# A gated linear-attention and mixer kernel on one core: a new written order for all engines

## The chip, the core and the metric

The kernel runs on one NeuronCore of a Trainium2 chip. Five engines work side by side: TensorE (PE in the profile) multiplies matrices, VectorE (DVE) and ScalarE (ACT) do elementwise work and can read PSUM, GpSimd (POOL) does elementwise work in SBUF only, and SyncE (SP) issues DMA transfers; ACT can issue them too. Each engine works through its own queue in the order in which the program was written, and waits on semaphores for what the others make.

The metric is the time on the device, in microseconds (us), of one execution. The kernel before took 165.89 us in the median of three runs (165.33 to 166.85).

## The reference

Two stages follow each other. The first is a recurrence over time with a state of 48 x 48 for each of 4 x 8 batches and heads; the second is a mixer over tokens and then over channels.

```python
for t in range(S):                                  # S = 768, D = 48
    state = alpha[:, :, t, :, None] * state + np.einsum('bhd,bhe->bhde', k[:, :, t], v[:, :, t])
    y[:, :, t] = np.einsum('bhd,bhde->bhe', q[:, :, t], state)

x = y.transpose(0, 2, 1, 3).reshape(B, S, H * D)    # B = 4, H * D = 384
xt = x.transpose(0, 2, 1)
h = np.maximum(xt @ w_tok1, 0.0) @ w_tok2           # 768 -> 256 -> 768 tokens
u = x + h.transpose(0, 2, 1)
out = u + np.maximum(u @ w_ch1, 0.0) @ w_ch2        # 384 -> 1536 -> 384 channels
```

All inputs and the output are float32 in DRAM; the kernel computes its products in bfloat16 and sums them in float32.

## The kernel before

**Attention in blocks.** Each batch has 3 blocks of 256 tokens, so blocks 0 to 2 belong to batch 0, 3 to 5 to batch 1, up to block 11. The recurrence of a block is written as products: sums of logs of alpha give decay factors, keys are multiplied by the inverse factor and queries by the factor, and a masked product of the two takes the place of the loop. A block works in two halves of 128 tokens (half 0 and half 1), and the state goes from half to half.

**Names.** A step has a short name and the number of its block or batch. For a block n:

- `ld_at`, `ld_qt`, `ld_kt`, `ld_vt`: the loads of alpha, queries, keys and values, 384 KB each, into one of 20 buffers of the class `in`.
- `ln` (blocks 0 to 2, one log 768 wide), or `ln1`, `P`, `lnP`, `r1` (later blocks: a log, a product of neighbouring alphas, its log, a reciprocal).
- `cumw` or `cum`: PE sums the logs. `E`, `Et`, `IE`: ACT takes exponentials of the sum, of the block's total, and of the negative sum.
- `qq`, `ql`, `kk`, `kl`: queries times E, keys times IE, each as two pieces 384 wide in the first blocks.
- `trq`, `trk`, then `evq`, `evk`: PE transposes them, DVE or ACT copies them out of PSUM (from block 6 on a transposing DMA, `dq`, `dk`, does it, and `pq` a copy).
- `vb`: the cast of the values; `vs0`, `vs1`: copies of its halves to the other partitions, written after `K`; `ka`, `kb`, `kc`: the same for keys, from block 3 on.
- `K`: keys times values. `s`, `sa`, `sm`: the new state, from K, the old state and the decay.
- `G0`, `G1`, `mask0`, `mask1`: the two products of keys and queries, and the masks that DVE lays over them; `ia`, `ib`: queries times state; `y0`, `y1`: masked product times values; `x0`, `x1`: the copy of the result to SBUF.

For a batch: `t1` (first token weight, six products each for two tiles), `ht` (relu), `t2_b_i` (second token weight), `u` (add), `up`/`ut` (transpose), `c1` and `rt` (first channel weight, relu), `c2` and `o` (second channel weight, add), `st` (store). `ldw` and `cw` load and cast the weight pieces; `cw_wt20` is the first half of the second token weight, which `t2_0_0` reads first.

**What sets the order.** Nothing is scheduled when the kernel is built. `build` describes all steps with what they need; `run` then walks through the string `ORDER`, in which every step stands once with a letter for its engine (t PE, s ACT, v DVE, g POOL, y SP), and emits them in that order. `BUFS` gives, in the order of first use, the buffer number of every value. So the order of a queue, the engine of a copy and the buffer are all written out. Semaphores make each step wait for what it reads, and a step that writes a buffer waits for the last readers of what stood there.

**Port order.** Steps of DVE and POOL that are marked as using a shared port (the scalings, casts, shifts, `P`, `k0a`, `q0r`) also wait for each other: where one of them follows one of the other engine in the written order, it waits until that has ended. This is `shared`:

```python
if last and last[0] != e:
    self.tc.add_manual_dep(i.ins, last[1].ins.name, ...)
self.port_last = (e, i)
```

**Unread products.** `f1_...` and `f3_...` are 1 or 3 products of a zero tile with 512 columns into a PSUM bank that nobody reads before it is overwritten. They are optional (`filler`, `fill`): each stands ahead of a step of PE, if the order names it.

Of the kernel before, what the change touches and what calls it, by code (L numbers as in the profile page):

```python
# [892 lines left out]
```

## Time and profile before

| | |
|---|---|
| median of three runs | 165.89 us (165.33 to 166.85) |
| the profiled execution, whole | 165.84 us |
| its span, first to last instruction | 164.1 us |
| PE busy | 155.5 us (95%) |
| DVE, ACT, POOL busy | 110.8, 101.1, 75.5 us |
| mean granted TensorE clock | 0.990 |
| read from and written to DRAM | 25.17 MB, 4.72 MB |

A row of a timeline or of a group names the line of the kernel, the engine, the operation and what it writes and reads. An idle time in square brackets at the end of a row is how long the engine stood still ahead of it, and what ended that. A row of a list of waits has the total, the number and the longest. A row of a stretch has its length, then the busy time of PE, PE's weight loads, DVE, ACT and POOL with the number of instructions, then the granted clock, the DMA engines' share and GB/s. Lines that many steps share: L604 is every attention product of PE, L666 the transposes, L697 and L698 the copies of ACT and of DVE and POOL, L653 the scalings, L810 the products t2, L829 and L834 c1 and c2. A row of a DMA ends with the time from its issue to its landing.

### The profile page before, as it was taken

The page shows a single profiled execution, that of the slowest core. Times are in us where ns is not written, and L with a number is a line of the kernel's source. Part 1 is how long each engine was busy: PE and PEld are TensorE (multiplying, and loading weights), DVE is VectorE, ACT ScalarE, POOL GpSimd, SP SyncE. Part 2 cuts the span into 40 slices and gives each one's busy share as a digit, 9 for nine tenths or more (in the row PEclk, how much of TensorE's full clock was granted, in tenths as well). Part 3 has the DMA queues.
Part 4 walks back from the last instruction along what each step waited for, and adds up shares of the span by engine and source line. Part 5 has one row for each costly group of instructions (what it writes and reads, how often), then busy time and mean ns, then how long its engine had stood idle before and what let it go on. Part 6 is the DMA issues. An engine that isn't in the chain of part 4 may idle for free.

```text
span 164.1 us, 4068 instructions
## 1 busy us (share of the span) xinstructions
PE 155.5 (95%) x1601; PEld 98.2 (60%) x1601; DVE 110.8 (68%) x197; ACT 101.1 (62%) x188; POOL 75.5 (46%) x94
## 2 busy tenths in 40 slices
PE   7959889899999999999999999999999999999992
PEld 2444656576657676665667666666566665566660
DVE  4056999689699777967789998874591283524341
ACT  3698798998998786289995947466615101562000
POOL 4054489972942827289795494739700000000000
PEclk9995999999999999999999999999999999999999
DMA  4999999999999998999999999699012135220314
GB/s 127 324 318 321 248 340 279 348 348 344 342 363 336 291 265 202 249 302 211 239 239 174 234 184 221 144 221 248 19 48 100 48 68 129 90 98 9 113 71 143
DMA packets 76322, 34.46 MB, mean 210 GB/s; under 512 B 68112, under 2 KB 76304, under 8 KB 76304
## 3 DMA queue, kind: packets, MB, share of 16 engines
q1 hardware_dynamic: 64704, 27.73, 66.5%
q10 hardware_dynamic: 11600, 6.49, 13.7%
q8 instruction: 12, 0.20, 0.5%
q14 instruction: 6, 0.05, 0.1%
HBM read 25.17 MB, written 4.72 MB: 182 GB/s over the span
## 4 chain that ended last, share of the span: by engine, by line
PE 52%; DVE 4%; ACT 2%; ACTq 1%; issue 1%
PE ps L834 22%; PE ps L829 19%; PE ps L604 6%; PE ps L805 3%; PE ps L810 2%; DVE u L814 1%; ACTq L545 1%; DVE o L838 1%; DVE pkk L653 1%; DVE ut L698 1%; ACT vb L697 0%; ACT ut L697 0%; DVE rt L802 0%; DVE ss L762 0%; ACT lf L592 0%
## 5 line engine op out<-in xcount | busy, mean ns | idle before, releaser
L834 PE MATMUL ps<-wc,rt 128*128 128x384 bf16 (+2 forms) x300 | 54.7, 320 | 0.0
L829 PE MATMUL ps<-ut,wc 128*128 128x384 bf16 x288 | 51.8, 326 | 0.3 <-ACT E L631 0.2
L800 ACT ACTIVATE rt<-ps 128x384 bf16<-128x384 f32 x55 | 25.3, 493 | 24.6 <-PE ps L829 24.5
L829 PEld LDWEIGHTS <-wc 128*128 128x128 bf16 x288 | 27.0, 98 | 17.7 <-issue 1.2
L834 PEld LDWEIGHTS <-rt 128*128 128x128 bf16 x300 | 27.6, 98 | 16.6
L802 DVE TENSOR_SCALAR rt<-ps 128x384 bf16<-128x384 f32 x41 | 21.6, 552 | 14.4 <-PE ps L829 13.9
L720 DVE TENSOR_TENSOR gtm<-ps,mk 128x1024 bf16<-128x1024 f32 x24 | 28.3, 1217 | 2.7 <-PE ps L604 2.5
L653 POOL TENSOR_TENSOR pkk<-in,IE 128x384 bf16<-128x384 f32 (+1 forms) x12 | 14.3, 1206 | 9.4 <-DVE pkq L653 6.3
L838 DVE TENSOR_TENSOR o<-ps,u 128x384 f32<-128x384 f32 (+2 forms) x25 | 13.3, 535 | 6.1 <-PE ps L834 6.0
L814 DVE TENSOR_TENSOR u<-ps,x 128x384 bf16<-128x384 f32 x24 | 12.3, 552 | 4.6 <-PE ps L810 4.5
L653 POOL TENSOR_TENSOR pkq<-in,E 128x384 bf16<-128x384 f32 (+1 forms) x8 | 11.2, 1408 | 7.0 <-DMA in<-in_moe_w_ch_dram 3.8
L697 ACT CAST x<-ps 128x384 bf16<-128x384 f32 x19 | 9.0, 481 | 7.7 <-PE ps L604 7.7
L697 ACT CAST vb<-in 64x384 bf16<-64x384 f32 (+1 forms) x18 | 11.8, 658 | 2.4 <-DMA in<-in_v_dram 1.6
L698 POOL CAST vb<-in 64x384 bf16<-64x384 f32 (+1 forms) x17 | 9.5, 559 | 7.0 <-issue 3.2
L805 PE MATMUL ps<-x,wt 128*128 128x384 bf16 x48 | 11.4, 326 | 0.3 <-ACT x L697 0.3
L604 PE MATMUL ps<-zs 128*128 128x512 bf16 x28 | 9.9, 495 | 1.1 <-DVE zs L507 1.1
L810 PE MATMUL ps<-ht,wt 128*128 128x384 bf16 x48 | 10.1, 326 | 0.7 <-ACT wt L697 0.7
L589 POOL TENSOR_TENSOR in<-in 128x384 f32<-128x384 f32 x9 | 9.0, 1000 | 3.4 <-DMA in<-in_alpha_dram 2.5
L653 DVE TENSOR_TENSOR pkq<-in,E 128x384 bf16<-128x384 f32 (+1 forms) x9 | 6.0, 689 | 6.5 <-ACT E L637 4.6
L645 POOL TENSOR_TENSOR in<-in,in 128x384 f32<-128x384 f32 x7 | 7.0, 1001 | 5.4 <-DVE in L649 3.0
L768 DVE TENSOR_TENSOR tmp<-ps,ss 128x384 f32<-128x384 f32 x12 | 6.6, 554 | 3.5 <-POOL ss L771 1.8
L604 PE MATMUL ps<-tpq,tpk 48*64 48x128 bf16 (+1 forms) x288 | 8.3, 221 | 0.3 <-ACT tpk L697 0.2
(93 smaller groups left out, 212.2 us busy)
## 6 DMA issues: line engine op xcount, KB each, us to landing
in<-in_alpha_dram SPq DMA_DIRECT2D x11, 384.0 KB, 6.3
in<-in_q_dram SPq DMA_DIRECT2D x10, 384.0 KB, 5.2
in<-in_moe_w_ch_dram SPq DMA_DIRECT2D x10, 384.0 KB, 7.3
in<-in_k_dram SPq DMA_DIRECT2D x9, 384.0 KB, 5.8
in<-in_v_dram SPq DMA_DIRECT2D x9, 384.0 KB, 6.0
out_dram<-o SPq DMA_DIRECT2D x14, 192.0 KB, 2.4
out_dram<-o ACTq DMA_DIRECT2D x9, 192.0 KB, 1.9
in<-in_moe_w_tok_dram SPq DMA_DIRECT2D x3, 384.0 KB, 5.6
```

The costliest lines, as they stand in the source:

```text
L604: return self.pe.matmul(out, lhsT=lhsT, rhs=rhs, start=start, stop=stop, skip_group_check=True)
L653: self.shared(self.eng[e].tensor_tensor(self.t(dst)[:, c : c + z, :, 0:D], self.t(src)[:, :, c : c + z, :].rearrange("p h s d -> p s h d") ...
L697: return self.act.copy(d, s)
L720: self.nc.vector.tensor_tensor(self.t(gtm)[:, hf, :, :], self.pair(gp).rearrange("p a (j t) -> p (a j) t", t=128), bass.AP(tensor=m.tensor ...
L800: self.act.activation(d, s, AF.Relu)
L802: self.nc.vector.tensor_scalar_max(d, s, 0.0)
L805: self.pe.matmul(self.bank(bank)[:, 0:HD], lhsT=self.wt1[:, kc, m * 128 : m * 128 + 128], rhs=self.t(x), start=(kc == 0), stop=(kc == NS - 1))
L810: self.pe.matmul(self.bank(bank)[:, 0:HD], lhsT=self.wt2[:, kc, i * 128 : i * 128 + 128], rhs=self.t(hts[kc]), start=(kc == 0), stop=(kc = ...
L814: self.nc.vector.tensor_tensor(self.t(u)[:, i % 3], self.bank(bank)[:, 0:HD], self.t(x), ALU.add)
L829: self.pe.matmul(self.bank(bank)[:, 0:HD], lhsT=self.wc1[:, kc, mc * 128 : mc * 128 + 128], rhs=self.t(ut)[:, 3 * half : 3 * half + 3, kc, ...
L834: self.pe.matmul(self.bank(bank)[:, 0 : cz - ca], lhsT=self.t(rts[mc][0])[:, i * 128 : i * 128 + 128], rhs=self.wc2[:, mc, ca:cz], start=( ...
L838: self.nc.vector.tensor_tensor(self.t(o)[:, ca:cz], self.bank(bank)[:, 0 : cz - ca], self.t(u)[:, i % 3, ca:cz], ALU.add)
```

## The change

`ORDER` and `BUFS` are new from end to end; no function changes. The steps and their work are the same, but for the unread products: ten groups (22 products) instead of twelve (28). Of the steps, 137 change their engine or issuing queue: 29 transfers between SP and ACT, the rest among DVE, ACT and POOL. The head of the two orders, up to the first t2 step:

```diff
-f3_trk0t f1_trq0t f3_trq0t f3_cumw1t f3_cumw0t ld_at0y ln0s ld_at1y ln1s ld_qt0y ld_kt0y ld_vt0y cumw0t E0s ql0v
-ld_at2y f1_K0t f3_K0t cumw1t qq0v trq0t ld_kt1y ld_vt1y IE0s IE1s evq0v ld_qt1y Et0s vb0s kk0g E1s ld_at3y kl0g trk0t
-ln2s Et1s evk0s K0t kk1g kl1g s0_0v cumw2t vb1s vs0_0s Et2s E2s IE2s ld_qt2y vs1_0g qq1v ql1v sa1_0t ln13s f1_trq1t
-G0_0t sm1_0v f3_trq1t G1_0t K1t P3g ld_kt2y ld_vt2y lnP3s trk1t trq1t sa0_1t evk1s evq1s ld_kt3y qq2g mask0_0v
-mask1_0v ldw_wt10y ld_vt3y sm0_1v cum3t y0_0t x0_0s ib0t sa1_1t f3_trq2t ld_at4y ld_qt3y ql2v trq2t sm1_1v kl2v E3s
-IE3s kk2g vs0_1g ldw_wt11s y1_0t evq2v G0_1t ia1t kk3g f1_G11t ldw_wt20y ldw_wt21y mask0_1v k0a3g x1_0s G1_1t ld_kt4y
-vb2s trk2t mask1_1v ldw_wc10y r13s ib1t K2t evk2s sa0_2t sm0_2v G0_2t cw_wt10s mask0_2v kl3g ldw_wc11y vs1_1g vs0_2g
-vs1_2s ka3s vb3s f3_G12t G1_2t kb3s ldw_wc13y t1_0_1_0t y0_1t trk3t ld_at5y y1_1t cw_wt11g ib2t ia2t ln14s mask1_2v
-y0_2t x0_1v x0_2v x1_1s vs1_3s vs0_3s ld_qt4s ldw_wc12y kc3g t1_0_1_1t y1_2t t1_0_0_0t t1_0_1_2t P4g t1_0_0_1t
-t1_0_0_2t t1_0_0_3t t1_0_0_4t q0r3g x1_2v t1_0_0_5t t1_0_1_3t evk3v qq3g t1_0_1_4t ql3g lnP4s t1_0_1_5t k0a4g ht_0_0s
-cw_wt20s K3t ht_0_1v cum4t cw_wt21s t2_0_0t t2_0_1t IE4s s0_3v sa1_3v u_0_0v t2_0_2t kk4g ldw_wc15y trq3t u_0_1v
...
+f1_cumw1t f1_K0t f3_cumw1t ld_at0y ln0s ld_at1y ln1s f3_cumw0t f3_K0t ld_kt0y ld_at2y cumw0t f3_trq0t f1_trk0t cumw1t
+ld_qt0y ld_vt0y E0s ql0v IE0s qq0v ld_kt1s ld_vt1y E1s trq0t ld_qt1y ld_at3y kl0g kk0g ld_qt2y Et0s Et1s evq0v vb0v
+trk0t K0t evk0v IE1s ld_kt2y ln2s vs1_0s ld_kt3y s0_0v cumw2t vb1g f1_G00t kk1v ql1v qq1v sa1_0t kl1g G0_0t sm1_0v
+vs0_0g mask0_0v P3g IE2s Et2s E2s ln13s ld_vt2s G1_0t K1t trk1t ld_vt3s lnP3s sa0_1t trq1t ql2g qq2g evk1s kk2g
+mask1_0v y0_0t ib0t cum3t vs0_1s evq1s ldw_wt10y IE3s sm0_1v sa1_1t f3_trq2t trq2t ldw_wt11y ld_at4y y1_0t E3s vs1_1s
+sm1_1v x0_0v G0_1t kl2g evq2v ld_qt3y trk2t mask0_1v x1_0s ldw_wt20y vb2s evk2s G1_1t ia1t ldw_wt21y ib1t k0a3g kl3g
+kk3g y0_1t K2t r13s vb3s vs0_2s sa0_2t mask1_1v vs1_2g ka3g G0_2t f3_G12t G1_2t sm0_2v cw_wt10g cw_wt11g y1_1t ld_kt4y
+ib2t ia2t P4g x1_1s mask0_2v trk3t t1_0_1_0t y0_2t t1_0_1_1t t1_0_0_0t mask1_2v ldw_wc10y y1_2t t1_0_0_1t vs1_3s x0_1s
+vs0_3s x0_2v kc3g x1_2s ldw_wc11y t1_0_1_2t ldw_wc13s evk3v kb3s lnP4s q0r3g t1_0_1_3t ln14s ld_qt4s ld_at5y t1_0_1_4t
+t1_0_1_5t qq3g ht_0_1v ql3g t1_0_0_2t cw_wt20s t1_0_0_3t t1_0_0_4t t1_0_0_5t k0a4g ht_0_0v K3t ldw_wc15y cum4t IE4s
+s0_3v ld_vt4y t2_0_0t E4s cw_wt21s r14s sa1_3v kk4g kl4g u_0_0v t2_0_1t t2_0_2t trq3t evq3s u_0_1v t2_0_3t cw_wc10s
...
```

The end of the two orders:

```diff
-c2_3_3_2t c2_3_0h1_3t o_3_1v st_3_1y o_3_5v o_3_4v c2_3_3_3t c2_3_0h0_1t st_3_5y st_3_4y o_3_0h1v st_3_0h1y o_3_3v
-c2_3_0h0_2t c2_3_0h0_3t o_3_0h0v st_3_0h0y st_3_3s
...
+rt_3_10_1v c2_3_4_2t c2_3_4_3t c2_3_0h1_3t o_3_0h1v o_3_4v c2_3_5_2t st_3_0h1s c2_3_5_3t c2_3_3_1t c2_3_3_2t c2_3_3_3t
+o_3_5v st_3_4s o_3_1v o_3_3v st_3_1y st_3_5s st_3_3y c2_3_0h0_0t c2_3_0h0_1t c2_3_0h0_2t c2_3_0h0_3t o_3_0h0v
+st_3_0h0y
```

Three things in words. The first loads were alpha 0, alpha 1, queries 0, keys 0, values 0, alpha 2; they become alpha 0, alpha 1, keys 0, alpha 2, queries 0, values 0. ACT issues 5 of the loads ahead of `t2_0_0` instead of 2. The copy `evk0`, the cast `vb0` and `kk1` go to DVE; `ql2`, `kl2`, `vb1` and `vs0_0` to POOL; `vs1_0`, `vs0_1`, `vs1_1`, `vs0_2`, `x0_1` and `x1_2` to ACT. In `BUFS`, the keys of blocks 0 and 1 now share one of the three buffers for scaled keys (`kk1` and `kl1` wait until PE has read those of block 0).

105 lines of the change are left out of this document (52 added, 53 removed), and 22 rows, old and new, of the table BUFS.

## The prediction

> **What bounds the kernel now.** I read the busy shares first, then stretches cut where PE's waits end, then PE's waits.
>
> ```profile
> PE 155.5 (95%) x1601; PEld 98.2 (60%) x1601; DVE 110.8 (68%) x197; ACT 101.1 (62%) x188; POOL 75.5 (46%) x94
> ```
> ```profile
> 28.58:31.29 2.71, 1.99 (x21) 1.25 (x20) 1.79 (x4) 2.67 (x6) 2.71 (x4) 1.00 1.12 339
> 32.30:160.90 128.60, 128.08 (x1281) 82.07 (x1280) 89.38 (x153) 75.26 (x147) 56.37 (x62) 1.00 0.77 193
> 160.90:164.10 3.20, 0.00 (x0) 0.00 (x0) 0.49 (x1) 0.00 (x0) 0.00 (x0) 1.00 0.31 113
> ```
> ```profile
> PE ps L666 <- POOL pkk L653: 1.7, 1, 1.7
> PE ps L604 <- DVE zs L507: 1.1, 1, 1.1
> PE ps L810 <- ACT wt L697: 0.7, 1, 0.7
> PE ps L604 <- ACT la L595: 0.5, 1, 0.5
> ```
>
> The second number of a stretch is PE's busy time. From 32.30 us to 160.90 us PE stands still for 128.60 - 128.08 = 0.52 us, and the last 3.20 us are one DVE add and its store. So the end of the kernel is the time at which the head (all work up to the first product of the second token weight, t2_0_0, which started at 31.29 us) is through, plus PE work that no order can shorten. The instructions of PE ahead of t2_0_0 are the same in both orders apart from the unread products, and so are those behind it. The forecast is therefore the shift of t2_0_0, plus waits that come or go behind it.
>
> The head is not bound by PE: but for the 1.1 us for the zeros that open the kernel, its waits above are for a scaled key, a weight cast and a log.
>
> **The change part by part.**
>
> *Unread products.* 28 become 22.
>
> ```profile
> 1.06 5.11 PE L604 MATMUL ps<-zs 128*128 128x512 bf16 x13 [1.06 <-DVE zs L507]
> 14.91 1.17 PE L604 MATMUL ps<-zs 128*128 128x512 bf16 x3
> 4.37 0.84 ACT L598 ACTIVATE la<-in 128x768 bf16<-128x768 f32 x1 [2.28 <-DMA in<-in_alpha_dram]
> 6.00 0.65 PE L604 MATMUL ps<-la,u 128*128 128x384 bf16 x3
> ```
>
> Ahead of the first sum 11 stand instead of 13, 5.11 / 13 = 0.39 us each: the sum starts near 5.4 us instead of 6.00, and not before 5.21 us, when its log is done. Nothing comes of it, since the next step now waits for a load (below). Three fewer (4 to 1) stand between block 0's state and block 1's keys, at 1.17 / 3 = 0.39 us; they filled a wait there. The sixth lay in one too. Value: 0; bounds, 0 and -6 x 0.39 = -2.3 us.
>
> *Keys of block 0 ahead of its queries.* The load in third place was issued at 1.94 us and took 4.9 us, the one in fifth place 5.24 and 4.0 us.
>
> ```profile
> 1.94 1.17 SPq L545 DMA_DIRECT2D in<-in_q_dram  x1
> in<-in_q_dram SPq DMA_DIRECT2D x1, 384.0 KB, 4.9
> ...
> 5.24 0.37 SPq L545 DMA_DIRECT2D in<-in_v_dram  x1
> in<-in_v_dram SPq DMA_DIRECT2D x1, 384.0 KB, 4.0
> ```
> ```profile
> 7.91 1.03 DVE L653 TENSOR_TENSOR pkq<-in,E 128x384 bf16<-128x384 f32 x2 [4.57 <-ACT E L637]
> 9.08 1.96 POOL L653 TENSOR_TENSOR pkk<-in,IE 128x384 bf16<-128x384 f32 x2 [6.34 <-DVE pkq L653]
> 11.09 0.62 PE L666 MATMUL ps<-idn,pkk 128*128 128x128 bf16 x8 [1.70 <-POOL pkk L653]
> ```
>
> Queries go from third to fifth place: from 6.84 us to 9.24 us. The keys land early but do not run early: POOL's key scaling waited for DVE's query scaling (the row of 9.08 us), a wait that shared() makes from the written order, and in the new order kl0 and kk0 still follow qq0. So queries 9.25 + 1.03 = 10.3 us, keys + 1.96 = 12.3 us, their transpose at 12.35 us instead of 11.09: **+1.26 us** on the first chain. Queued behind the wait on POOL are vb1 and kl1.
>
> *Engines of copies, from there to t2_0_0.* Three chains run.
>
> ```profile
> 11.64 0.52 PE L604 MATMUL ps<-vb,pkk 64*128 64x96 bf16 x16
> 13.53 0.48 PE L604 MATMUL ps<-ss,idn 128*128 128x384 bf16 x1
> 14.38 1.03 DVE L653 TENSOR_TENSOR pkq<-in,E 128x384 bf16<-128x384 f32 x2 [1.56 <-POOL vb L698]
> 15.79 2.34 DVE L720 TENSOR_TENSOR gtm<-ps,mk 128x1024 bf16<-128x1024 f32 x2
> 20.66 1.32 DVE L698 COPY tpq<-ps 128x1024 bf16<-128x1024 bf16 x1 [0.22 <-PE ps L666]
> 26.86 1.48 DVE L698 CAST x<-ps 128x384 bf16<-128x384 f32 x3
> 28.25 0.69 DVE L698 COPY tpk<-ps 128x1024 bf16<-128x1024 bf16 x1
> ```
>
> DVE: the key copy evk0, now on DVE, 13.05 to 13.73 us; state s0_0, then kk1, ql1, qq1 at 0.52 us each (1.03 / 2) to 15.8 us, the second pair done at 15.4 us before. sm1_0 and two masks (2.34 us) end at 18.7 us (18.13 before). POOL: kl1 waits for qq1, 16.85; vs0_0 0.5; P3 18.35; ql2 and qq2, both on POOL now, 20.3 us. The query copy evq2 then runs from 20.95 to 22.25 us (21.98 before). Two masks 24.6, sm0_2 25.1, two masks 27.5 us (26.94 before). So +1.26 us has shrunk to +0.55: DVE gave ql2, kl2 and a net two of its casts to x away.
>
> ```profile
> 18.26 0.99 ACT L697 COPY tpk<-ps 128x1024 bf16<-128x1024 bf16 x1
> 19.15 1.32 ACT L697 COPY tpq<-ps 128x1024 bf16<-128x1024 bf16 x1
> 20.31 0.49 ACT L697 CAST x<-ps 128x384 bf16<-128x384 f32 x1
> 20.68 0.54 ACT L631 ACTIVATE E<-ps 128x400 f32<-128x400 f32 x1
> 21.80 0.89 ACT L697 CAST vb<-in 128x768 bf16<-128x768 f32 x1
> 22.54 0.58 ACT L601 ACTIVATE lf<-lf 128x384 f32<-128x384 f32 x1
> 30.41 1.55 ACT L697 CAST wt<-in 128x768 bf16<-128x768 f32 x2
> 31.29 1.15 PE L810 MATMUL ps<-ht,wt 128*128 128x384 bf16 x6 [0.67 <-ACT wt L697]
> ```
>
> ACT: start to start its pieces take 0.89 us (key copy), 1.16 (query copy), 0.37 (384 wide), 0.74 (768 wide). vs1_0 now stands ahead of block 2's exponentials and waits for the product K0, which ends near 13.45 us (12.1 before); the sum behind K0 took 1.4 us at half clock, so IE2, Et2 and E2 are through at 16.7 us, ln13 and two issues of loads at 17.9 us, and lnP3 waits for P3 until 18.35 us (17.83 before). Behind it: evk1 0.89, evq1 1.16, vb2 and vb3 0.74 each, evk2 0.89 and, with lnP3, twelve pieces of 0.37 are 8.9 us, so ACT comes to x1_2 at 27.2 us. x1_2 has to wait for the last mask and its product, 27.8 us. From its start, x1_2 takes 0.37, then stand a load issue (0.4), kb3, lnP4 and ln14 (1.1), another issue (0.4) and the cast of the weight, 0.85: **31.0 us**. ht_0_0, on DVE instead of ACT, is done by 30 us and no longer holds the cast up. t2_0_0: 31.05 us instead of 31.29, **-0.25 us**. Its weight has to have landed by 30.1 us: loads number 20 in both orders, and before it had landed ahead of 30.41 us, where the cast follows ACT's own work. Bounds: if nothing of the first chain's delay is caught up, +1.26 us; if DVE's shorter list alone counts, -1.6 us (second rival).
>
> *Loads moved to ACT's queue.* Five are issued by ACT ahead of t2_0_0 (kt1, vt2, vt3, wc13, qt4) instead of two.
>
> ```profile
> 41.92 0.37 ACTq L569 DMA_DIRECT2D in<-in_moe_w_ch_dram  x1
> 42.36 0.46 ACTq L545 DMA_DIRECT2D in<-in_v_dram  x1
> 45.01 3.04 SPq L545 DMA_DIRECT2D in<-in_alpha_dram  x2
> ```
>
> On ACT such issues took 0.37 and 0.46 us, one right behind the other; on SP two took 3.04 us. I take 0.4 us, ACT's own rows; the upper end is 1.5 us each (third rival). SP's wt10 now waits until POOL has read vt's buffer (vs0_0, 17.35 us) against an issue at 17.8 us before; as many loads are out by then, so I count no shift.
>
> *From t2_0_0 to the end.* PE keeps the same products in a changed order; buffers in PSUM and SBUF are dealt anew. Of the 0.52 us of waits some go, some come: +0.1 us, bounds -0.5 and +1.2 us, the upper end a wait like each of the two of 0.5 and 0.7 us above, once more. At the end the order of the last stores changes, but again 4 products of 320 columns, one add and one store close it: 3.20 us, no change.
>
> The sum: the profiled execution took 165.84 us (164.1 us span, 1.74 us around it), level with the median of 165.89. 165.84 - 0.25 + 0.1 = **165.7 us**.
>
> [...]
>
> ```profile
> 12.50:13.00 0.50, 0.50 (x3) 0.23 (x2) 0.32 (x1) 0.41 (x2) 0.50 (x2) 0.50 1.16 323
> 15.50:16.00 0.50, 0.50 (x3) 0.00 (x0) 0.50 (x2) 0.40 (x1) 0.00 (x0) 0.85 1.18 312
> ```
>
> A pause of 1.70 us (9.4 to 11.1 us) was followed by half clock from about 12.2 to 15.7 us. [...]
>
> **The rivals.**
>
> *The first chain's delay passes through.* For it: every step up to 16.85 us is 0.4 to 1.3 us late, and ACT now waits for K0. Against it: DVE's list is shorter. 165.84 + 1.26 = 167.1 us.
>
> *DVE's list is what counts.* Before, DVE ran from the query pair at 14.38 us to evk3 at 28.94 us almost without a gap. Now the pair starts 0.4 us later, and three pieces of 0.52 us have gone. Without waits for POOL, t2_0_0 would be 1.6 - 0.4 = 1.2 us earlier, 1.6 where K1, no longer waiting, also comes earlier by one unread product of 0.39 us; with the 0.52 us of waits behind it gone too, 165.84 - 1.6 - 0.5 = 163.7 us. Against it: ql2 and qq2 on POOL take 2 x 1.0 us, and evq2 waits for them; and ACT's 0.85 us cast comes last.
>
> *ACT's issues are held up as SP's are* (the other side). Place: vt2 and vt3, then wc13 and qt4, all ahead of the weight cast on the engine that ends last. It decides as soon as an issue on ACT takes longer than the 0.45 us that ACT stands idle ahead of lnP3. Price: four times 1.15 instead of 0.4 us (an SP issue took 1.17 us above), 3.0 less 0.45 = 2.55 us: 165.7 + 2.5 = 168.2 us, less where a load waits anyway. Against it: ACT's issues of before.
>
> **How the numbers follow.** Forecast (level, 164.6 to 166.8 us) 0.46; delay passes through 0.10; DVE's list 0.21; ACT held up 0.23. One per cent, about what a measurement tells from no change, is 1.66 us: faster is below 164.2 us, slower above 167.5. DVE's list falls on the fast side with a little of the forecast, 0.22; ACT held up and a part of the delay (0.04) on the slow side, 0.27; 0.51 between. The range goes from DVE's list to ACT held up, 163.7 to 168.2 us, as cases on both sides hold two thirds of what the forecast leaves.
>
> **What would show it.** In the changed kernel's profile: PE's first transpose of keys at 12.3 us with a wait for POOL; POOL's first keys waiting for DVE near 10.3 us; ACT idle near 11.5 to 13.5 us for K0; t2_0_0 (first L810) between 30.5 and 31.6 us, its wait on ACT's cast; PE's idle time behind it under 1 us. Wrong would be t2_0_0 more than 1 us away from there, issues on ACT over 0.6 us, or a PE wait of over 1 us behind 32 us, for a load above all.

## The result and the profile after

The changed kernel took 168.18 us in the median (166.62 to 170.94, 20 runs), the kernel before 165.61 us (165.02 to 166.85, 20 runs): slower, with a ratio of 1.013 and a 95% interval of 1.011 to 1.015. The forecast was 165.7 us. The ratios and their intervals here leave out the slow executions, those over 1.5% above the kernel's fastest (3 of these 20), and are not quotients of the medians given beside them. The profiled execution of the changed kernel took 166.87 us (165.1 us span), so it is one of its short ones: about 1.3 us of the median do not show in it.

The page's busy times of the changed kernel, then stretches of both. Columns are as before: length, busy time of PE, PE's weight loads, DVE, ACT, POOL, then the clock.

```profile
PE 155.5 (94%) x1595; PEld 99.4 (60%) x1595; DVE 114.2 (69%) x203; ACT 99.0 (60%) x188; POOL 74.2 (45%) x88
```
```profile
8.00:12.00 4.00, 1.33 (x13) 0.72 (x12) 2.29 (x3) 2.39 (x5) 1.61 (x2) 0.95 1.17 325
12.00:16.00 4.00, 3.60 (x35) 1.97 (x35) 3.25 (x7) 0.96 (x2) 1.16 (x2) 0.50 1.17 325
16.00:20.00 4.00, 3.73 (x62) 3.03 (x62) 3.37 (x4) 2.88 (x6) 3.75 (x5) 0.70 1.16 320
...
32.08:161.86 129.78, 129.35 (x1286) 83.24 (x1286) 92.58 (x158) 76.64 (x151) 53.96 (x55) 1.00 0.75 191
```

The kernel before:

```profile
8.00:12.00 4.00, 2.30 (x45) 1.67 (x43) 2.24 (x3) 3.77 (x8) 2.13 (x3) 1.00 1.15 318
12.00:16.00 4.00, 4.00 (x34) 1.59 (x28) 2.18 (x5) 3.76 (x6) 2.28 (x3) 0.57 1.17 322
...
31.29:160.87 129.58, 129.09 (x1286) 82.60 (x1286) 90.00 (x153) 76.27 (x148) 57.30 (x63) 1.00 0.77 195
```

From the start of t2_0_0 to PE's end this execution needs 129.78 us instead of 129.58: nearly the same. The head has lost 0.79 us. From 8 to 16 us ACT works 3.35 us instead of 7.53 and POOL 2.77 instead of 4.41: the changed order has little for them to do until block 0's state is made, and what they did there before comes later. From the clock column, the time at half clock in the three stretches is (1 - 0.95) x 4 / 0.5 = 0.4 us, 4.0 us and 2.4 us, 6.8 us together, where the kernel before has 0.43 x 4 / 0.5 = 3.4 us.

PE's waits and the head's chain in the changed kernel:

```profile
PE ps L666 <- DVE pkq L653: 1.8, 1, 1.8
PE ps L666 <- POOL pkk L653: 1.2, 2, 0.7
PE ps L810 <- ACT wt L697: 0.6, 1, 0.6
```
```profile
9.22 1.03 DVE L653 TENSOR_TENSOR pkq<-in,E 128x384 bf16<-128x384 f32 x2 [5.88 <-DMA in<-in_q_dram]
10.39 1.95 POOL L653 TENSOR_TENSOR pkk<-in,IE 128x384 bf16<-128x384 f32 x2 [7.65 <-DVE pkq L653]
12.40 0.60 PE L666 MATMUL ps<-idn,pkk 128*128 128x128 bf16 x4 [0.42 <-POOL pkk L653]
13.82 0.51 ACT L697 CAST vb<-in 64x384 bf16<-64x384 f32 x1 [3.38 <-PE ps L604]
16.11 1.00 POOL L653 TENSOR_TENSOR pkk<-in,IE 128x384 bf16<-128x384 f32 x1 [2.28 <-PE ps L604]
17.17 0.50 POOL L698 CAST vb<-in 64x384 bf16<-64x384 f32 x1
17.75 1.00 POOL L589 TENSOR_TENSOR in<-in 128x384 f32<-128x384 f32 x1
18.78 0.52 ACT L595 ACTIVATE la<-in 128x384 bf16<-128x384 f32 x1 [1.10 <-POOL in L589]
...
22.86 0.51 ACT L697 CAST vb<-in 64x384 bf16<-64x384 f32 x1
23.27 0.47 ACT L697 CAST x<-ps 128x384 bf16<-128x384 f32 x1
23.77 0.83 ACT L697 CAST vb<-in 128x768 bf16<-128x768 f32 x1
...
29.34 0.48 ACT L697 CAST x<-ps 128x384 bf16<-128x384 f32 x1
31.21 0.81 ACT L697 CAST wt<-in 128x768 bf16<-128x768 f32 x1
32.08 1.15 PE L810 MATMUL ps<-ht,wt 128*128 128x384 bf16 x6 [0.63 <-ACT wt L697]
```

The first three rows came as forecast (9.24, 10.3, 12.35 us). Then kl1 (16.11 us), vs0_0 (17.17) and P3 (17.75) stand one behind the other on POOL. The row of kl1 names PE as what ended its wait; the queries of block 1 on DVE (qq1), which kl1 follows in the port order, ended at 15.85 us, 0.26 us ahead of it, and a run below shows that it is these that it waits for. lnP3 waits for P3 (18.78); and ACT works almost without a gap (busy for 11.98 of 12.43 us) from there to the cast cw_wt20 (31.21), for which t2_0_0 waits.

### The profile page after: what moved, and what is told of

The parts are those of the page before. It is cut to its first block, busy times and chain, and to the rows that moved or that the text cites. A ratio compares the mean times of both kernels' runs of the same rounds, so it can differ in the third digit from the quotient of the medians.

```text
span 165.1 us, 4036 instructions
## 1 busy us (share of the span) xinstructions
PE 155.5 (94%) x1595; PEld 99.4 (60%) x1595; DVE 114.2 (69%) x203; ACT 99.0 (60%) x188; POOL 74.2 (45%) x88
## 4 chain that ended last, share of the span: by engine, by line
PE 77%; ACT 7%; POOL 5%; DMA 3%; DVE 2%; SPq 2%; issue 1%; ACTq 1%; POOLq 0%; DVEq 0%
PE ps L834 29%; PE ps L829 25%; PE ps L604 13%; PE ps L810 5%; PE ps L805 4%; POOL pkk L653 3%; DMA in<-in_q_dram 3%; SPq L545 2%; PE ps L666 2%; POOL pkq L653 1%; ACT wc L697 1%; DVE u L814 1%; PE ps L821 1%; ACT rt L800 1%; ACT tpq L697 1%
## 5 line engine op out<-in xcount | busy, mean ns | idle before, releaser
L829 PE MATMUL ps<-ut,wc 128*128 128x384 bf16 x288 | 52.2, 326 | 0.2
L800 ACT ACTIVATE rt<-ps 128x384 bf16<-128x384 f32 x51 | 23.2, 491 | 31.3 <-PE ps L829 25.8
L829 PEld LDWEIGHTS <-wc 128*128 128x128 bf16 x288 | 27.1, 98 | 16.7 <-issue 0.5
L802 DVE TENSOR_SCALAR rt<-ps 128x384 bf16<-128x384 f32 x45 | 23.7, 553 | 15.3 <-PE ps L829 14.6
L653 POOL TENSOR_TENSOR pkk<-in,IE 128x384 bf16<-128x384 f32 (+1 forms) x13 | 16.1, 1255 | 10.9 <-DVE pkq L653 7.7
L697 ACT CAST vb<-in 64x384 bf16<-64x384 f32 (+1 forms) x24 | 14.6, 616 | 3.7 <-PE ps L604 3.4
L653 POOL TENSOR_TENSOR pkq<-in,E 128x768 bf16<-128x768 f32 (+1 forms) x9 | 13.0, 1454 | 6.7 <-DVE in L649 5.4
L589 POOL TENSOR_TENSOR in<-in 128x384 f32<-128x384 f32 x8 | 8.0, 999 | 10.1 <-PE ps L604 5.6
L645 POOL TENSOR_TENSOR in<-in,in 128x384 f32<-128x384 f32 x8 | 8.0, 1001 | 2.1 <-ACT x L697 1.2
L604 PE MATMUL ps<-vb,gtm 128*128 128x48 bf16 x192 | 8.6, 183 | 0.3 <-DVE gtm L720 0.3
L604 PE MATMUL ps<-tpq,tpk 48*64 48x128 bf16 (+1 forms) x288 | 8.5, 224 | 0.2 <-DVE u L814 0.2
L771 POOL TENSOR_TENSOR ss<-tmp,E 128x384 bf16<-128x384 f32 x7 | 5.9, 837 | 6.3 <-PE ps L829 3.0
L604 PE MATMUL ps<-zs 128*128 128x512 bf16 x22 | 7.6, 487 | 1.1 <-DVE zs L507 1.1
```

Source lines behind the costliest of these rows:

```text
L604: return self.pe.matmul(out, lhsT=lhsT, rhs=rhs, start=start, stop=stop, skip_group_check=True)
L653: self.shared(self.eng[e].tensor_tensor(self.t(dst)[:, c : c + z, :, 0:D], self.t(src)[:, :, c : c + z, :].rearrange("p h s d -> p s h d") ...
L697: return self.act.copy(d, s)
L800: self.act.activation(d, s, AF.Relu)
L802: self.nc.vector.tensor_scalar_max(d, s, 0.0)
L829: self.pe.matmul(self.bank(bank)[:, 0:HD], lhsT=self.wc1[:, kc, mc * 128 : mc * 128 + 128], rhs=self.t(ut)[:, 3 * half : 3 * half + 3, kc, ...
```

## The experiments

The expectations name theories: A, the order of the head alone; B, the two issuing queues make it vary; C, ACT's queue stops at the issues of wc23 and wc24; D, the place of the cast cw_wt20; E, an unread product on the path; G, a gate near 51 us from loads behind t2_0_0; H, kk1 and kl1 behind s0_0 make P3 late; H2, one chain from P3 on sets t2_0_0. The kernel before ran anew beside each set of runs, with medians from 165.04 to 165.77 us, so ratios compare better than microseconds.

### Single parts of the head

Each starts from the changed kernel. The five loads that ACT issues ahead of t2_0_0 go back to SP (picked out of the list):

```diff
-ld_kt1s ld_vt2s ld_vt3s ldw_wc13s ld_qt4s
+ld_kt1y ld_vt2y ld_vt3y ldw_wc13y ld_qt4y
```

> The changed order with the five loads that ACT issues ahead of t2_0_0 (kt1, vt2, vt3, wc13, qt4) issued by SP at the same places. Theory B expects the median to fall by 1 us or more, to about 167 us, and the spread to shrink to under 1 us. Theory A expects no change within 0.4 us, or slower by up to 1 us where SP's queue, held at wt10 for a free buffer until 17.7 us, holds vt2 and vt3 too.

Measured: 168.01 us, ratio 1.012 (1.008 to 1.017); t2_0_0 at 32.17 us. These issues are not the cause.

The load order of block 0 as before:

```diff
-ld_kt0y ld_at2y cumw0t f3_trq0t f1_trk0t cumw1t ld_qt0y ld_vt0y E0s
+ld_qt0y ld_kt0y cumw0t f3_trq0t f1_trk0t cumw1t ld_vt0y ld_at2y E0s
```

> The changed order with the first loads as before: queries, keys and values of block 0 ahead of alpha of block 2. Theory A expects the query scaling to start near 7.2 us instead of 9.22 and the first transposed keys near 10.5 us instead of 11.44 and 12.40 (two halves), t2_0_0 earlier by 0.3 to 1.0 us and the time shorter by as much, about 167.4 us. Theory B expects the same median within 0.4 us.

Measured: 167.9 us, 1.012 (1.008 to 1.017). PE's transposes of keys came at 9.32 and 10.28 us, 2.1 us earlier, and t2_0_0 at 32.62 us, later still.

The keys not only loaded but run ahead of the queries:

```diff
-E0s ql0v IE0s qq0v
+IE0s kl0g kk0g E0s ql0v qq0v
...
-trq0t ld_qt1y ld_at3y kl0g kk0g ld_qt2y Et0s Et1s evq0v vb0v trk0t K0t evk0v
+trk0t trq0t ld_qt1y ld_at3y ld_qt2y Et0s Et1s evk0v vb0v K0t evq0v
```

> The changed order, loads as in it, but the keys of block 0 also scaled, transposed and copied ahead of its queries (IE0, kl0, kk0 ahead of E0, ql0, qq0; trk0 ahead of trq0; evk0 and vb0 ahead of evq0). Theory A with the port's order as the cost expects POOL's first scaling near 7.2 us instead of 10.39, K0 near 11.5 us instead of 12.99, t2_0_0 earlier by 0.3 to 0.8 us and about 167.5 us. Theory B expects no change within 0.4 us.

Measured: 167.3 us, 1.009 (1.006 to 1.013); the first transposes at 8.12 us, 3.3 us earlier, t2_0_0 at 32.47. Three rows of the run before (queries_first):

```profile
13.11 0.82 POOL L698 CAST vb<-in 128x768 bf16<-128x768 f32 x1 [2.89 <-DMA in<-in_v_dram]
15.72 1.00 POOL L653 TENSOR_TENSOR pkk<-in,IE 128x384 bf16<-128x384 f32 x1 [1.79 <-DVE pkq L653]
27.93 0.48 ACT L697 CAST x<-ps 128x384 bf16<-128x384 f32 x1 [1.15 <-PE ps L604]
```

Neither run moved t2_0_0 forward, but neither shows what the first chain is worth, since other delays took its place. The cast vb1, which kk1 follows, now waits for its load until 13.1 us in both, so P3 starts only 0.40 and 0.45 us earlier than in the changed kernel. Then ACT's copy x1_1 waits 1.15 and 1.05 us for PE, which was slow until about 21 us (products of 384 columns at 20.66 and 20.61 us took 0.48 us each, against 0.33 at 18.59 us in the changed kernel; the mean granted clock was 0.967 in both), where it waits 0.20 us in the changed kernel. The row of kl1 (15.72 us) settles its wait: PE's product sa1_0, the one ahead of kl1 in the list, had ended at 14.4 us, and kl1 started 0.26 us behind the end of qq1 on DVE, as in the changed kernel.

One group of unread products left out (it stood ahead of trq2, which was ready):

```diff
-sm0_1v sa1_1t f3_trq2t trq2t
+sm0_1v sa1_1t trq2t
```

> The changed order without the three unread products ahead of block 2's query transpose (f3_trq2), which in its profile run from 20.71 to 21.35 us while the scaled queries are ready at 20.66 us. Theory E: they stand on the head's path here; expects the transpose 0.6 us earlier, the masks behind it and t2_0_0 earlier by 0.4 to 0.6 us, and as much off the median. The rival (DVE or ACT is what binds there) expects t2_0_0 within 0.2 us of 32.1 us.

Measured: 168.26 us, 1.017 (1.012 to 1.021); t2_0_0 at 32.12 us. No gain.

The cast that t2_0_0 waits for moved from ACT to DVE:

```diff
-evk3v kb3s
+evk3v cw_wt20v kb3s
...
-ql3g t1_0_0_2t cw_wt20s t1_0_0_3t
+ql3g t1_0_0_2t t1_0_0_3t
```

> The changed order with the cast of the first half of the second token weight moved from ACT, where it stands behind x1_2, two load issues and three more pieces, to DVE behind evk3. Theory D: t2_0_0 is late in the changed order by this place in ACT's queue, whatever the first chain does (it started at 32.1 to 32.6 us in four profiles, each time 0.63 us after the rest was ready). It expects PE's wait for the cast gone, t2_0_0 near 31.5 us, and 0.4 to 0.6 us off the median of 168.0. The rival (what is late in the head is late ahead of the cast) expects PE to wait for the relu ht_0_0 instead and under 0.2 us off.

Measured: 167.99 us, 1.015 (1.012 to 1.019). PE in this run:

```profile
31.15 1.14 PE L810 MATMUL ps<-ht,wt 128*128 128x384 bf16 x6
33.15 0.62 PE L666 MATMUL ps<-idn,pkq 128*128 128x128 bf16 x8 [0.87 <-DVE u L814]
51.40 1.62 PE L829 MATMUL ps<-ut,wc 128*128 128x384 bf16 x9 [1.44 <-ACT rt L800]
```

t2_0_0 is 0.93 us earlier and has no wait; 0.35 us of that is P3's earlier start in this execution (17.40 us). Right behind t2_0_0 the transpose of block 3's queries waits 0.87 us. The profile names DVE's add; POOL's scaling of those queries (31.14 to 33.10 us in this run) is what ended just ahead of it. Another wait follows at 51.4 us. In this execution the head is late on ACT and on POOL at once.

### The issues on ACT behind t2_0_0

The changed kernel once more:

> The changed kernel unchanged, to see how far its executions lie apart and what another profile of it shows. The profile on hand took 166.87 us, 1.3 us less than the median of 168.18: its t2_0_0 started 0.79 us later than before, and PE stood still 0.23 us longer behind it. Theory A (the head's order alone, the same in each execution) expects a spread of under 1 us and t2_0_0 within 0.3 us of 32.08 us. Theory B (loads in two queues land at varying times) expects a spread of 2 us or more, and in a longer execution waits of PE for a load or for a step behind one, in the head or between 32 and 60 us.

Measured: 168.01 us, 1.011 (1.006 to 1.016). Its profiled execution took 167.92 us, 1.05 us more than the first. PE's starts agree to 0.25 us up to 50 us; then it stands 1.01 us. ACT and PE in this execution, then ACT in the first:

```profile
49.11 1.43 ACTq L569 DMA_DIRECT2D in<-in_moe_w_ch_dram  x2
50.58 0.87 ACT L800 ACTIVATE rt<-ps 128x384 bf16<-128x384 f32 x2 [1.39 <-PE ps L604]
51.51 1.62 PE L829 MATMUL ps<-ut,wc 128*128 128x384 bf16 x9 [1.01 <-ACT rt L800]
```
```profile
48.41 0.37 ACTq L569 DMA_DIRECT2D in<-in_moe_w_ch_dram  x1
48.82 0.51 ACTq L569 DMA_DIRECT2D in<-in_moe_w_ch_dram  x1
49.38 0.87 ACT L800 ACTIVATE rt<-ps 128x384 bf16<-128x384 f32 x2 [0.32 <-issue]
```

The two issues are wc23 and wc24. They began 0.7 us later and took 1.43 us together instead of 0.88; the relus behind them in ACT's queue started 1.2 us later, and PE stood for them. The relu's row names PE's L604 as what ended its wait, but the relus read c1 (L829), and they started 0.04 us behind the end of the second issue here and in no_fill_q2, and 0.05 us behind it in head_before_rest_after. PE's wait near 51 us is 0.54 to 1.44 us long in three other profiles above (loads_on_sp, no_fill_q2, wt20_on_dve); the first profile, queries_first and keys_run_first have none. So this is one place where the kernel's executions part.

Both issues moved to SP:

```diff
-mask1_4v ldw_wc23s ld_kt5y ia4t cw_wc14g ldw_wc24s
+mask1_4v ldw_wc23y ld_kt5y ia4t cw_wc14g ldw_wc24y
```

> The changed order with the loads wc23 and wc24 issued by SP instead of ACT, at the same places. Theory C: ACT's queue stops at these two until an earlier load has landed (in a profile of 167.92 us ACT stood still for 1.39 us there and PE then for 1.01 us for a relu, in one of 166.87 us neither), so most executions pay up to 1.3 us for it. It expects no PE wait for a relu near 50 us, the median near 166.9 us and the spread under 1.5 us. The rival (the head alone, and the spread has another source) expects 168.0 us as before.

Measured: 168.42 us, 1.020 (1.018 to 1.023). PE:

```profile
55.29 0.62 PE L666 MATMUL ps<-idn,pkk 128*128 128x128 bf16 x8 [0.57 <-DVE pkk L653]
59.91 0.36 PE L604 MATMUL ps<-vb,gtm 128*128 128x48 bf16 x8 [0.25 <-POOL vb L698]
68.11 1.46 PE L810 MATMUL ps<-ht,wt 128*128 128x384 bf16 x8 [0.76 <-ACT E L631]
```

The wait at 51 us is gone, and 1.6 us of others have come: the load of the keys of block 5 (kt5), behind wc23 in SP's queue, is issued at 48.34 us instead of 40.37, and the alphas behind it at 50.44 instead of 45.90. Theory C had 166.9 us for this run.

The other way round, the kernel before with these two issues on ACT:

```diff
-vs1_4g ldw_wc23y mask0_4v rt_0_9_1s rt_0_11_0s mask1_4v ldw_wc24y
+vs1_4g ldw_wc23s mask0_4v rt_0_9_1s rt_0_11_0s mask1_4v ldw_wc24s
```

> The kernel before with the loads wc23 and wc24 issued by ACT instead of SP, at the same places: theory C's step alone. Theory C expects ACT to stand still at them, and 0.5 to 1.3 us more than the median of the kernel before (165.7 us), with a wider spread. The rival expects no difference over 0.3 us.

Measured: 165.23 us, 1.000 (0.998 to 1.003). Theory C had 0.5 to 1.3 us more for this. In the profile the two issues took 0.38 and 0.37 us, so in this list they were not held up at all: it is not the engine alone that makes them long.

kt5 moved ahead as well, with the two issues on SP:

```diff
-ld_qt5y rt_0_2_1v
+ld_qt5y ld_kt5y rt_0_2_1v
...
-ldw_wc23s ld_kt5y ia4t cw_wc14g ldw_wc24s
+ldw_wc23y ia4t cw_wc14g ldw_wc24y
```

> The changed kernel with the two expert weights' loads wc23 and wc24 issued by SyncE as in the run that moved them alone, and the load of kt5 moved to directly behind qt5, five loads earlier. Theory G in the form that loads of keys late in SyncE's queue are what the moved issues delayed: the wait of 0.57 us near 55 goes and the whole is 166.8 to 167.2. Theory that any place makes another load late: a new wait of 0.5 us or more for at7 or at6 or behind, and 168 us.

Measured: 167.22 us, 1.008 (1.005 to 1.011). Against wc_on_sp, 1.020, the place of one load of 384 KB is worth over 1%, and the wait near 55 us is gone: theory G holds for it. The profiled execution, at 168.44 us the longest of the eight, is late in the head, which is the same as the changed kernel's:

```profile
14.49 0.82 POOL L698 CAST vb<-in 128x768 bf16<-128x768 f32 x1 [1.98 <-DMA in<-in_v_dram]
```

The cast vb1 waits for its load and starts at 14.49 us, where it started at 13.00 in the first profile; P3 follows at 18.74 us and t2_0_0 at 33.33. This is a second place where executions part.

All of the loads number 33 to 48 in the order of the kernel before, in the same slots of the list (the first lines of the edit):

```diff
-ldw_wc22s ln15s c1_0_3_0t c1_0_10_1t ldw_wc20s
+ld_qt5y ln15s c1_0_3_0t c1_0_10_1t ld_kt5y
...
-mask1_4v ldw_wc23s ld_kt5y ia4t cw_wc14g ldw_wc24s
+mask1_4v ldw_wc23y ldw_wc24y ia4t cw_wc14g ldw_wc25s
...
```

> The changed kernel with its loads number 33 to 48 in the order and on the issuing queues of the kernel before, in the same slots of the list. Theory G: the wait near 51 us goes, none over 0.5 us behind 32.5 takes its place, 166.4 to 166.9, ratio 1.003 to 1.007. If the gate comes from the products' order and not from the loads': the wait near 51 stays at about 1 us, and the time at 168.

Measured: 168.76 us, 1.017 (1.013 to 1.021), not better, where theory G had 166.4 to 166.9 us. SP's queue shows one difference from the kernel before:

```profile
40.67 8.68 SPq L569 DMA_DIRECT2D in<-in_moe_w_ch_dram  x3
```

Three weight loads held SP up for 8.7 us, where the three of the kernel before took 3.50 us from 41.41 us on. That alone is not the cost: in kt5_early three took 8.64 us, with a ratio of 1.008. In the profile of loads_as_before PE has no wait over 0.23 us behind t2_0_0, as theory G had it, and still needs 130.89 us from there to its end instead of 129.78. What costs the rest stays open.

### The two halves

These kernels take the order up to t2_0_0 from one kernel and the rest from the other. First the head of before:

```diff
-f1_cumw1t f1_K0t f3_cumw1t ld_at0y ln0s ld_at1y ln1s f3_cumw0t f3_K0t ld_kt0y ld_at2y cumw0t f3_trq0t f1_trk0t cumw1t
...
+f3_trk0t f1_trq0t f3_trq0t f3_cumw1t f3_cumw0t ld_at0y ln0s ld_at1y ln1s ld_qt0y ld_kt0y ld_vt0y cumw0t E0s ql0v
...
```

> The kernel before's order, engines and buffers up to t2_0_0, and the changed kernel's behind it (three buffers are other ones). Theory D (only the place of the cast cw_wt20 in ScalarE's queue, ahead of t2_0_0): t2_0_0 starts near 31.3 us as before and the whole is as before, 165.2 to 165.9 us. Theory G (a gate near 51 us that the load order behind t2_0_0 sets, whatever the head): t2_0_0 near 31.3, PE's waits behind it 0.8 us or more, the first for ScalarE's relus near 51, and 167 us or more, ratio 1.008 to 1.014.

Then the changed head:

```diff
-f3_trk0t f1_trq0t f3_trq0t f3_cumw1t f3_cumw0t ld_at0y ln0s ld_at1y ln1s ld_qt0y ld_kt0y ld_vt0y cumw0t E0s ql0v
...
+f1_cumw1t f1_K0t f3_cumw1t ld_at0y ln0s ld_at1y ln1s f3_cumw0t f3_K0t ld_kt0y ld_at2y cumw0t f3_trq0t f1_trk0t cumw1t
...
```

> The changed kernel up to t2_0_0, and the kernel before's order behind it (five buffers are other ones). Theory D: t2_0_0 near 32.1 and 0.8 to 1.0 us more than before, 166.4 to 166.7. Theory G with D: the same, 166.4, with no PE wait over 0.5 us behind 32.5, and a small spread; so G alone is worth what the changed kernel has beyond this one, 1.2 to 1.8 us. If neither holds and the head costs more by what it leaves late, 168.

| head | rest | median | ratio |
|---|---|---|---|
| before | before | 165.66 us | |
| before | changed | 166.73 us | 1.004 (1.001 to 1.007) |
| changed | before | 166.99 us | 1.007 (1.005 to 1.010) |
| changed | changed | 168.18 us | 1.013 (1.011 to 1.015) |

0.4 and 0.7 per cent add up to 1.1 of the 1.3: there is a loss on each side of t2_0_0. PE with the head of before, then ACT and PE with the changed one:

```profile
50.59 1.62 PE L829 MATMUL ps<-ut,wc 128*128 128x384 bf16 x9 [0.69 <-ACT rt L800]
```
```profile
31.98 1.15 PE L809 MATMUL ps<-ht,wt 128*128 128x384 bf16 x6 [0.64 <-ACT wt L696]
42.21 0.83 ACT L696 CAST wc<-in 128x768 bf16<-128x768 f32 x1 [1.14 <-DMA in<-in_moe_w_ch_dram]
43.48 2.11 PE L828 MATMUL ps<-ut,wc 128*128 128x384 bf16 x12 [0.92 <-ACT rt L799]
```

The wait near 51 us comes with the changed rest, t2_0_0 near 32 us with the changed head; with the head of before it started at 31.80 us in this execution, as P3's load came 0.8 us later than in the first profile of the kernel before. The wait at 43.48 us is in neither kernel: wc12, loaded in the head of before and behind it in the changed one, stands at the very end of the head in this mix, and ACT's cast of a channel weight at 42.21 us waits 1.14 us for its load. Of the four profiles of this mix two have such a wait, so 0.7% is rather an upper value for the head.

The head of before, the changed rest, with wc23 and wc24 on SP and kt5 early as above:

```diff
-ld_qt5y rt_0_2_1v
+ld_qt5y ld_kt5y rt_0_2_1v
...
-ldw_wc23s ld_kt5y ia4t cw_wc14g ldw_wc24s
+ldw_wc23y ia4t cw_wc14g ldw_wc24y
```

> The kernel before up to t2_0_0, the changed kernel's order behind it, with wc23 and wc24 issued by SyncE and the load of kt5 directly behind qt5. The same without these two edits measured 166.73 us, 1.07 more than before. Theory G (those issues and late keys of block 5 are what the changed order costs behind t2_0_0): 165.6 to 166.0, no PE wait over 0.4 us behind 32 us. Rival (other places of the changed order cost as much): 166.5 to 167 and a wait elsewhere.

Measured: 166.21 us, 1.002 (0.999 to 1.006), no longer to be told from the kernel before, with no PE wait over 0.4 us behind 32 us. From 1.004 that is no proof by itself. With kt5_early and the waits it speaks for theory G in the second half; loads_as_before, which has both edits too and gained nothing, shows that they are not the whole of it.

### Inside the head

The engines alone: before's order with the changed engines and queues of 23 steps (ten of them, picked out of the list).

```diff
-vb0s evk0s kk1g vb1s kl2v ql2v vs0_0s vs1_0g x1_2v ht_0_0s
+vb0v evk0v kk1v vb1g kl2g ql2g vs0_0g vs1_0s x1_2s ht_0_0v
...
```

> The kernel before with its own order throughout, but with the changed kernel's engines and issuing queues for the 23 instructions up to t2_0_0 that have others there (qt of nothing moved). The run with the changed kernel's head and before's rest measured 1.33 us more than before. Theory H (kk1 and kl1, the keys of block 1, come to stand behind s0_0 in the shared port order and delay P3 on GpSimd by about 1 us; that is order and engine together): by the engines alone kl1 stays where it was, t2_0_0 within 0.3 us of before's 31.3 and the whole 165.4 to 165.9. Rival (the moved copies and casts themselves load GpSimd): t2_0_0 at 32 and 166.6 to 167.2.

The changed order with before's engines, the same edit from the other side:

```diff
-vb0v evk0v kk1v vb1g kl2g ql2g vs0_0g vs1_0s x1_2s ht_0_0v
+vb0s evk0s kk1g vb1s kl2v ql2v vs0_0s vs1_0g x1_2v ht_0_0s
...
```

> The changed kernel's order up to t2_0_0 with the kernel before's engines and queues, and before's order behind it. Theory H: most of the 1.33 us is here, t2_0_0 near 32 and 166.6 to 167.2. Rival (engines): 165.4 to 165.9. If both parts cost half, 166.2 to 166.5 in both runs.

Measured: 167.76 us, 1.014 (1.009 to 1.019), and 167.77 us, 1.017 (1.012 to 1.023). Each alone comes out worse than both together (1.007, 1.005 to 1.010). PE with the changed engines, then with the changed order:

```profile
13.31 1.04 PE L666 MATMUL ps<-idn,pkk 128*128 128x128 bf16 x8 [3.92 <-POOL pkk L653]
32.28 0.81 PE L805 MATMUL ps<-x,wt 128*128 128x384 bf16 x4 [0.76 <-ACT x L697]
```
```profile
15.49 1.12 PE L603 MATMUL ps<-la,u 128*128 128x384 bf16 x3 [1.79 <-ACT la L597]
26.39 0.37 PE L603 MATMUL ps<-vb,gtm 128*128 128x48 bf16 x8 [0.60 <-DVE gtm L719]
```

With the engine letters but not their places PE waits 3.9 us for POOL's keys; with the places but not the letters it waits 1.8 us for ACT's log. None of the forecasts that I had written down was right.

kk1 and kl1 put ahead of s0_0, from here on with the changed head and before's rest:

```diff
-ld_kt3y s0_0v cumw2t vb1g f1_G00t kk1v ql1v qq1v sa1_0t kl1g
+ld_kt3y kk1g kl1g s0_0v cumw2t vb1g f1_G00t ql1v qq1v sa1_0t
```

> The run with the changed kernel's head and before's rest (166.99 us), with kk1 and kl1, the keys of block 1, on GpSimd directly after vs1_0 and ahead of s0_0, cumw2 and vb1 in the list, about as in the kernel before. Theory H: P3 on GpSimd starts near 16.8 instead of 17.7 us, the logarithm behind it on ScalarE 17.9 instead of 18.8, t2_0_0 near 31.3, and 165.7 to 166.3 us. Rival (the head is late by the half clock and the late transposes of keys alone): P3 earlier but t2_0_0 still at 32, and 166.8 to 167.1.

Measured: 167.26 us, 1.013 (1.008 to 1.018). P3 came later instead of earlier, at 18.21 us:

```profile
16.48 1.03 DVE L652 TENSOR_TENSOR pkq<-in,E 128x384 bf16<-128x384 f32 x2 [2.27 <-POOL vb L697]
17.63 0.50 POOL L697 CAST vb<-in 64x384 bf16<-64x384 f32 x1 [1.18 <-issue]
```

kk1 waited 1.43 us for PE, yet kl1 was through at 15.68 us, 1.4 us earlier than in the changed kernel. But vb1, behind it on POOL, now held up the queries ql1 and qq1 on DVE, and vs0_0 waited for these in the port order, so P3's place was not tried. The profiles together show a pattern:

| kernels | P3 starts | t2_0_0 starts | between |
|---|---|---|---|
| changed head, its lists (7 profiles) | 17.66 to 17.89 us | 31.98 to 32.22 us | 14.32 to 14.34 us |
| kk1 and kl1 moved | 18.21 us | 32.55 us | 14.34 us |
| before's head (4 profiles) | 16.73 to 17.61 us | 30.90 to 31.80 us | 14.16 to 14.49 us |
| queries first, keys run first | 17.35, 17.30 us | 32.62, 32.47 us | 15.27, 15.17 us |
| kt5_early (changed head) | 18.74 us | 33.33 us | 14.59 us |
| head_engines, head_order | 19.14, 17.93 us | 33.74, 33.42 us | 14.60, 15.49 us |

In the kernel before P3 waits for its load; in the changed one it waits for kl1 and vs0_0. P3 in the kernel before:

```profile
16.80 1.00 POOL L589 TENSOR_TENSOR in<-in 128x384 f32<-128x384 f32 x1 [2.45 <-DMA in<-in_alpha_dram]
```

So one cast, vs0_0, was put behind P3:

```diff
-G0_0t sm1_0v vs0_0g mask0_0v P3g
+G0_0t sm1_0v mask0_0v P3g vs0_0g
```

> The run with the changed kernel's head and before's rest (166.99 us), with one instruction moved: vs0_0, the cast of 0.50 us that stands between kl1 and P3 on GpSimd, comes directly behind P3. In the profiles with the changed kernel's head and its own cast list, t2_0_0 starts 14.32 to 14.34 us after P3 starts, in all of seven. Theory H2 (one chain from P3 on sets t2_0_0): P3 at 17.1 to 17.2, t2_0_0 at 31.5, and 166.3 to 166.6 us. Rival (other chains, of GpSimd's queries or the late clock, stand equally late beside it): P3 0.5 us earlier, t2_0_0 less than 0.2 us earlier, 166.8 to 167.2.

Measured: 166.53 us, 1.006 (1.004 to 1.009).

```profile
16.77 0.99 POOL L588 TENSOR_TENSOR in<-in 128x384 f32<-128x384 f32 x1
31.10 1.15 PE L809 MATMUL ps<-ht,wt 128*128 128x384 bf16 x6 [0.63 <-ACT wt L696]
```

t2_0_0 follows P3 at 14.33 us again, 0.88 us earlier than without the edit (0.68 of it between kl1 and P3, from the edit, and 0.21 from kl1's earlier start in this execution). So H2 held for this run, which had 166.3 to 166.6 us. The time gains less than t2_0_0, 0.46 us by the medians, and the two ratios overlap.

Last, the changed kernel with vs0_0 behind P3, wc23 and wc24 on SP and kt5 early:

```diff
-G0_0t sm1_0v vs0_0g mask0_0v P3g
+G0_0t sm1_0v mask0_0v P3g vs0_0g
...
-ld_qt5y rt_0_2_1v
+ld_qt5y ld_kt5y rt_0_2_1v
...
-ldw_wc23s ld_kt5y ia4t cw_wc14g ldw_wc24s
+ldw_wc23y ia4t cw_wc14g ldw_wc24y
```

> The changed kernel whole, with the three small edits that the runs before point to: vs0_0 behind P3 on GpSimd, wc23 and wc24 issued by SyncE, and the load of kt5 directly behind qt5 (the last two alone measured 167.22 us, ratio 1.0077). If P3's place and these late issues are the two causes and they add: t2_0_0 at 31.1 to 31.3, no PE wait over 0.5 us behind 32 us, 165.8 to 166.4 us, ratio 1.002 to 1.005. If other places of the changed order cost as much: t2_0_0 early and new waits behind it that give it back, 166.8 to 167.4, ratio 1.006 to 1.010.

Measured: 167.38 us, 1.010 (1.005 to 1.015).

```profile
18.94 1.01 ACT L697 COPY tpk<-ps 128x1024 bf16<-128x1024 bf16 x1 [0.27 <-PE ps L666]
31.82 1.15 PE L810 MATMUL ps<-ht,wt 128*128 128x384 bf16 x6 [0.64 <-ACT wt L697]
66.09 1.46 PE L810 MATMUL ps<-ht,wt 128*128 128x384 bf16 x8 [0.29 <-ACT E L631]
```

The edits don't add up here. P3 starts at 17.12 us; then the copy evk1 waits for PE's transpose of block 1's keys, which runs at half clock in this execution (0.50 from 17.0 to 18.5 us), and t2_0_0 gains 0.26 us. At 66.1 us a further wait of 0.29 us takes that back. The waits found account for a part, not the whole. No kernel here was faster than the kernel before.

## Why the prediction was wrong

**The method.** The end as the start of t2_0_0 plus PE's fixed work plus waits behind it held: 129.78 us against 129.58 in the two profiled executions. The second profile of the changed kernel needs 130.71 us, with the wait of 1.01 us in it. The unread products' value of 0 held as far as it was tried (one group left out gained nothing), and so did the tail (3.2 us).

**The first chain.** Queries at 9.22 us (forecast 9.24), POOL's keys waiting for DVE, transposes at 12.40 (12.35): right. But more of this delay passes through than the sum had. Of the 1.3 us, 0.55 was to be left at P3 (end at 18.35 us instead of 17.80); 0.95 was left (start at 17.75 us instead of 16.80), and 0.79 at t2_0_0. In the changed kernel's profile the steps from the keys' transpose at 12.40 us to P3 follow each other with no gap over 0.26 us. No run took this delay away without putting another in its place, so its share is read from the profile and not shown by a run. The rival built on it, 167.1 us, lies nearer to the median; its price is for the head alone, and the median has a second loss behind t2_0_0.

**The ACT chain, the step that failed first.** The forecast had P3 end at 18.35 us, the log start there, x1_2 be reached at 27.2 us and the cast end at 31.0. Measured: 18.78, 29.34 and 32.0. P3 was 0.4 us late although DVE's qq1 ended as forecast (15.85 us for 15.8): the hand-overs had been put at next to nothing, and kl1 started 0.26 us behind qq1, vs0_0 0.06 behind kl1, P3 0.08 behind vs0_0. The mis-sized term is "twelve pieces of 0.37": start to start, the casts, copies and exponentials of 384 columns behind P3 took 0.38 (IE3, 21.94 to 22.32 us) to 0.54 us, as 0.41 (vs1_1, 22.86 to 23.27) and 0.50 (x1_0, 23.27 to 23.77), about 6.0 us together instead of 4.4, with x1_1's wait of 0.2 us for PE. From log to x1_2 10.56 us went by instead of 8.9. The kernel before has such pieces too, at 0.43 to 0.53 us from 27.64 to 29.61 us; the sum took the shortest of its rows. From x1_2 to the cast the sum had too much: 1.87 us went by instead of 2.27, as the two issues there (from 29.07 and 29.63 us) lay beside ACT's compute steps. So t2_0_0 came 0.79 us later than before, not 0.25 earlier. I also let DVE's shorter list carry weight: behind P3 it was ACT, and not DVE, that came last; its rival, 163.7 us, had nothing for it.

**Loads on ACT.** For the five ahead of t2_0_0, 0.4 us each was right (0.37 to 0.59), and moving them back gained nothing. The rival "ACT's issues are held up as SP's are" had the right mechanism in the wrong place: at wc23 and wc24 near 49 us, two of the 29 moved transfers, where they took up to 1.43 us with PE's relus behind them. PE stood 0.54 to 1.44 us for that where the rival had 2.5, so it is luck that its 168.2 us, the upper end of the range, meets the median of 168.18.

**From t2_0_0 to the end, the step that failed second.** +0.1 us was taken, with 1.2 as upper end. With the head of before, the changed rest measured 1.07 us by the medians, 0.7 us by the ratio (0.2 to 1.2 us by its interval). The wait that the runs showed there is PE's for the relus behind wc23 and wc24, in five profiles; the first profile of the changed kernel happens to show nothing of it. I had priced the head step by step and the other four fifths of the order by one sum of waits, although in the kernel before POOL and ACT waited for loads there (3.77 us up to 39.85 us, 2.79 us up to 68.93 us).

**The clock.** The kernel before ran at half clock for about 3.4 us, and the forecast added nothing for a longer stretch. The changed kernel's trace has 6.8 us of it. By the granted clocks about half the executions are like it (below), and the time does not tell them from the others.

**What stays open.** What the head still loses once P3 is early; which buffer or load held wc23 and wc24 up in each execution (their issues were seen to last, their releaser was not); why the loads in the order of before gained nothing; and how much of the spread from 166.6 to 170.9 us comes from the two places found (the issues near 49 us and the load of vb1 near 13 us), of which the kernel's two profiles show 166.87 and 167.92.

## What to carry to other kernels

What a step cost here was the lateness of what stood behind it in the same queue (0.68 us for P3 behind vs0_0): look over several profiles for an instruction whose start the end follows at a fixed distance (here P3, 14.3 us ahead of t2_0_0 in most profiles of the changed head), and price a new order by what is put in front of it. A row's releaser can be the wrong one of several: compare it with a run in which the named engine is early, as for kl1. A load issued by ACT cost nothing here as long as its issue took about 0.4 us; where two issues took 1.43 us, the compute steps behind them came 1.2 us later. A written order, its engines and its loads belong together: here the engine letters alone and the places alone each cost more than both. And price the long steady part of a reordered kernel too: one execution without waits there is not evidence that there are none.

## What was not expected of the hardware

In the kernels that begin as the kernel before does, the mean granted clock was below 0.983 in none of the 134 executions that enter the ratios and have their clock on record; in those that begin as the changed one does (block 0 and the keys of block 1 untouched) in 49 of 88. The two first profiles have 3.4 and 6.8 us at half clock. So a second stretch at half clock goes with a pause of PE near 10 us that is a little longer and has less work behind it (1.83 us, then 0.74 and 0.42, instead of 1.70), in about half the executions; with PE's wait of 3.92 us in head_engines all five executions were below 0.983. That the pause is the cause is not shown, since the orders differ in more. Within the changed kernels that had both, the executions with the lower clock were 0.1 us longer in the weighted mean, from 0.8 us shorter to 0.8 us longer by kernel: no difference that can be told, although PE loses 1.7 us of work in a further 3.4 us at half clock. That would fit other engines setting the pace there.
